# Query bits of the first head straight from PSUM into the stack, and warm products in TensorE's gaps up to the second exponential

## The chip, the cores and the metric

One core of one Trainium2 chip. The metric is the device time of one execution in microseconds (us) on that core. For each run the mean clock granted to TensorE over the execution is also known.

## The reference, cut to what matters

Attention over 4 batches, 8 heads, 768 positions, head width 64, in which a query sees only keys of the same hash bucket, and then a mixture of experts over its result.

```python
q_bits = (np.einsum('bhsd,dk->bhsk', q, proj) > 0)      # 6 bits for each position
k_bits = (np.einsum('bhsd,dk->bhsk', k, proj) > 0)
q_bucket = np.sum(q_bits * powers, axis=-1)             # ... k_bucket likewise
mask = q_bucket[:, :, :, None] == k_bucket[:, :, None, :]
scores = np.where(mask, scale * np.matmul(q, k.transpose(0, 1, 3, 2)), -1e9)
attn = np.exp(scores - np.max(scores, axis=-1, keepdims=True))
attn = attn / (np.sum(attn, axis=-1, keepdims=True) + 1e-09)
out = np.matmul(attn, v)
# ... then gating over 8 experts, relu(x @ w1) @ w2
```

## The kernel before

The mask is not applied to the scores. The bits are stacked as seven more rows below the 64 rows of k and q, so that one matmul with 71 rows gives a score that is far below zero where the buckets differ. Work goes in groups of four heads; a unit is a block of 128 keys of one head. Group 0 is prepared by `at_once()` before the loop:

```python
def at_once():
    bt = wk.tile([P, 2, S], F16, tag="t16", name="bt0")
    # ... hash_twice(): products of the transposed k or q with the hash table, into PSUM tile d["pr" + name]
    def move(name, h):                       # bits from bt into the stack, one half of the positions each
        for x in range(2):
            p = 64 * h + 32 * x
            pin(nc.vector.tensor_copy(d[name][D:KR, h, x * HT:(x + 1) * HT],
                                      bt[p:p + NB + 1, "kq".index(name), 0:HT]))
    # ... put(): bits of heads 2 and 3 to DRAM, from where SyncE fetches them
    for name in "kq":
        # ... transposes on VectorE, placements on ScalarE
        hash_twice(name, 1)
        warm_up(7 if name == "q" else 2)
        # ...
    k_, q_ = bt[:, 0, 0:HT], bt[:, 1, 0:HT]
    pin(nc.vector.tensor_scalar(k_, d["prk"][:, 0, 0:HT], 0.0, 0.5, op0=Alu.is_gt, op1=Alu.subtract))
    pin(nc.vector.tensor_scalar(k_, k_, BIG, None, op0=Alu.mult))
    move("k", 0)
    put("k")
    pin(nc.vector.tensor_scalar(q_, d["prq"][:, 0, 0:HT], 0.0, qoff[:, 0:1], op0=Alu.is_gt, op1=Alu.subtract))
    move("q", 0)
    put("q")
    place("q", 1, 1, nc.vector.tensor_copy)
    # ...
```

`warm_up(n)` issues n products of a tiny constant into a PSUM tile that nobody reads; they only keep TensorE busy. The later groups get their bits through DRAM, with transfers that SyncE issues in order, and the main loop runs one unit of scores ahead of the values:

```python
def prepare(n):                              # n > 0; a generator, run in pieces between units
    # ...
    put_bits()                               # bits to DRAM
    stack("k", 2)                            # rows of k, SBUF to SBUF
    # ...
    for h in range(1 if n < 3 else 0, 2):
        get_bits("k", h)                     # waits until the bits have landed in DRAM
        get_bits("q", h)
    stack("k", 3)
    stack("q", 2)
    get_bits("k", 2)
    # ...
    if n == 1:
        fetch(2, "kq")
        load_w(0, 1, pin=True, half=0)
    cast_v()
# ...
pts = {0: scores(*units[0])}
for u in range(len(units) + 1):
    if u < len(units):
        # ... pieces of prepare(n + 1)
        if u + 1 < len(units):
            pts[u + 1] = scores(*units[u + 1])       # two matmuls, then one exponential on ScalarE
    # ...
    if u > 0:
        values(*units[u - 1], pts.pop(u - 1))        # six matmuls; every sixth unit: normalisation on VectorE
```

The softmax here doesn't subtract the row's maximum and nothing guards it: scores larger than these inputs give would overflow.

## Time and profile before

| | kernel before |
|---|---|
| median of three first runs | 768.26 us (768.13 to 768.45) |
| the run that was profiled | 769.97 us, mean granted clock 0.995 |
| span in that profile | 768.3 us |
| TensorE (PE), ScalarE (ACT), VectorE (DVE), GpSimd (POOL) busy | 98%, 67%, 74%, 41% |

TensorE is busy nearly throughout, so what can be won is a gap at the beginning, where the first scores wait for their inputs, or clock.

Below, e0, e1, ... are the exponentials on ScalarE, one for each unit, and q is the moment at which q has arrived from DRAM (the third transpose on VectorE starts).

### The profile page before, as it was taken

Reading aid. Unit: us, or ns where it says so; the run is one execution under the profiler, and the core shown is the slowest. Engines: PE = TensorE matmul, PEld = TensorE weight load, DVE = VectorE, ACT = ScalarE, POOL = GpSimd, SP = SyncE. Lnnn points to the kernel's source line nnn. Section 1 sums busy time; section 2 is a strip of 40 time slices with the busy share of each in tenths; the row PEclk is TensorE's granted clock in tenths of the full one; section 3 lists DMA queues with packets and bytes.
Section 4 is the critical chain, followed back from the end, with each engine's and each line's share of the span. In section 5 each row is a group of like instructions: output and inputs, shape, how many; then the busy total and the mean of one; then the engine's idle time right before and its main releaser. Section 6 shows DMA issues by size and latency. Waiting matters only on the chain.

```text
span 768.3 us, 16720 instructions
## 1 busy us (share of the span) xinstructions
PE 749.8 (98%) x6285; PEld 518.2 (67%) x6285; DVE 565.6 (74%) x1261; ACT 515.1 (67%) x1027; POOL 318.6 (41%) x327
## 2 busy tenths in 40 slices
PE   8999999999999999999999999999999999999997
PEld 3665666566655667777777777777777777777664
DVE  6587766767579677777777777777777777777774
ACT  5886786678655777766666666666666666666661
POOL 6756444448300333434343334433543344324222
PEclk9899999999999999999999999999999999999999
DMA  7778448651030464676477647654964496443335
GB/s 229 191 199 188 133 113 212 150 144 41 2 55 1 83 110 84 112 136 110 83 132 130 118 89 137 119 104 83 164 118 90 91 169 113 84 83 83 83 83 138
DMA packets 41569, 88.08 MB, mean 115 GB/s; under 512 B 7232, under 2 KB 21840, under 8 KB 41488
## 3 DMA queue, kind: packets, MB, share of 16 engines
q0 software_dynamic: 27168, 69.49, 46.9%
q1 hardware_dynamic: 13324, 16.48, 8.1%
q10 hardware_dynamic: 996, 1.05, 0.6%
q8 instruction: 49, 0.80, 0.5%
q14 instruction: 32, 0.26, 0.1%
HBM read 53.05 MB, written 7.08 MB: 78 GB/s over the span
## 4 chain that ended last, share of the span: by engine, by line
PE 84%; ACT 7%; DVE 6%; issue 1%; DMA 1%; SPq 0%; ACTq 0%; DVEq 0%
PE a L824 18%; PE a L250 18%; PE d L824 13%; PE y L250 9%; PE st L567 6%; ACT pt L570 4%; PE d L250 4%; PE hp L644 4%; PE num L583 3%; PE yp L659 3%; PE pr L406 1%; PE hp L325 1%; PE yp L309 1%; ACT acc L241 1%; DVE hT L833 1%
## 5 line engine op out<-in xcount | busy, mean ns | idle before, releaser
L833 DVE CUSTOM_DVE_ANT_0 hT<-d,u 128x384 f16<-128x384 f32 x336 | 185.1, 552 | 96.7 <-ACT u L829 95.3
L254 ACT ACTIVATE vt<-a,p 128x256 f32<-128x256 f32 x324 | 153.6, 474 | 148.2 <-PE a L250 147.9
L570 ACT ACTIVATE pt<-st 128x768 f16<-128x768 f32 x192 | 147.4, 809 | 45.1 <-PE st L567 44.4
L829 ACT COPY u<-a 128x384 f32<-128x384 f32 x336 | 161.2, 480 | 23.4 <-PE a L824 19.8
L289 POOL DMA_DIRECT2D acc<-vt x72 | 62.0, 861 | 267.2 <-ACT vt L254 114.0
L250 PEld LDWEIGHTS <-hT 128*128 128x128 f16 x1296 | 126.3, 97 | 50.5 <-DVE hT L833 0.8
L250 PE MATMUL a<-t,hs 128*128 128x256 f16 x972 | 145.8, 273 | 2.2 <-ACT vt L254 1.0
L250 PEld LDWEIGHTS <-hs 128*128 128x128 f16 x972 | 94.8, 98 | 38.5 <-issue 2.8
L824 PEld LDWEIGHTS <-t 128*128 128x128 f16 x896 | 87.7, 98 | 36.4 <-issue 0.6
L824 PE MATMUL d<-xd,t 128*128 128x384 f16 x448 | 109.4, 326 | 0.3 <-DVE hT L833 0.3
L824 PE MATMUL a<-xT,s 128*128 128x384 f16 x448 | 109.4, 326 | 0.2
L567 PE MATMUL st<-qs,ks 71*128 71x384 f16 x384 | 95.8, 330 | 5.1 <-ACT pt L570 3.0
L250 PE MATMUL y<-t,hT 128*128 128x256 f16 x648 | 97.1, 272 | 0.0
L258 DVE SCALAR_TENSOR_TENSOR acc<-y,p,acc 128x256 f32<-128x256 f32 x162 | 77.3, 477 | 11.4 <-PE y L250 11.4
L134 POOL TENSOR_TENSOR t<-t 128x1024 f16<-128x1024 f16 (+1 forms) x39 | 81.9, 2108 | 0.1
L583 PEld LDWEIGHTS <-pt 128*128 128x128 f16 x1152 | 61.5, 98 | 27.0 <-issue 1.9
L824 PEld LDWEIGHTS <-s 128*128 128x128 f16 x672 | 65.5, 98 | 17.7 <-issue 2.5
L583 PE MATMUL num<-va,pt 128*128 128x65 f16 x1152 | 67.4, 195 | 0.3 <-ACT pt L570 0.3
L863 ACT ACTIVATE hT<-a 128x384 f16<-128x384 f32 x112 | 54.1, 483 | 1.8 <-PE a L824 1.7
L824 PE MATMUL a<-xd,s 128*128 128x384 f16 x224 | 54.3, 323 | 0.8 <-ACT u L829 0.8
L824 PE MATMUL d<-xT,t 128*128 128x384 f16 x224 | 54.7, 326 | 0.0
L824 PE MATMUL a<-xT,t 128*128 128x384 f16 x224 | 54.7, 326 | 0.0
(120 smaller groups left out, 946.8 us busy)
## 6 DMA issues: line engine op xcount, KB each, us to landing
acc<-vt POOLq DMA_DIRECT2D x72, 512.0 KB, 4.6
t<-in_moe_w_dram POOLq DMA_DIRECT2D x26, 512.0 KB, 8.0
v<-in_v_dram POOLq DMA_DIRECT2D x28, 192.0 KB, 5.6
out_dram<-acc SPq DMA_DIRECT2D x78, 64.0 KB
acc<-in_k_dram POOLq DMA_DIRECT2D x6, 768.0 KB, 6.1
acc<-in_q_dram POOLq DMA_DIRECT2D x6, 768.0 KB, 12.6
t<-in_moe_w_dram POOLq DMA_DIRECT2D x3, 1024.0 KB, 11.9
ks<-t SPq DMA_DIRECT2D x60, 48.0 KB
```

What stands on the lines that cost most here:

```text
L134: pin(nc.gpsimd.tensor_tensor(o[:, sl], x[:, sl], y[:, sl], op=op))
L250: pin(nc.tensor.matmul(dst, hq[hn][:, fo, :], wq[wn][:, fo, :], start=first and fo == 0, stop=fo == FH - 1, skip_group_check=True))
L254: pin(nc.scalar.activation(out=vt[:, k], in_=a, func=Act.Copy, scale=p))
L258: pin(nc.vector.scalar_tensor_tensor(out=dst, in0=src, scalar=p, in1=dst, op0=Alu.mult, op1=Alu.add))
L289: pin(nc.gpsimd.dma_start(out=acc[:, b, i], in_=vt, accum_op=Alu.add))
L567: pin(nc.tensor.matmul(st[:, i, 0:HT], d["k"][0:KR, h, kt * P:(kt + 1) * P], d["q"][0:KR, h, i * HT:(i + 1) * HT], start=True, stop=True))
L570: pin(nc.scalar.activation(out=pt, in_=st[:, :, 0:HT], func=Act.Exp, scale=scale))
L583: pin(nc.tensor.matmul(num[:, j * (D + 1):(j + 1) * (D + 1)], pf[:, j * P:(j + 1) * P], va[:, h, kt, :], start=(kt == 0 and j == 0), stop= ...
L824: pin(nc.tensor.matmul(bk, wq[wn][:, do, f * P:(f + 1) * P], xq[xn][:, do, :], start=first and do == 0, stop=do == 1, skip_group_check=True))
L829: pin(nc.scalar.copy(t, bk))
L833: pin(add(TENSOR_ADD_SAT, out=dst, in0=bk, in1=u, s0=3e38, s1=0.0))
L863: pin(nc.scalar.activation(out=hT[:, f, hi], in_=a, func=Act.Relu))
```

## The change

It has two intents. The bits of the first head of q, which the first scores wait for, are to come from PSUM by two small compares instead of one full compare and two copies. And TensorE's gaps up to the second exponential are to be filled with products, so that its clock doesn't drop just when it becomes the bound.

```diff
                 hash_twice(name, 1)
-                warm_up(7 if name == "q" else 2)
+                warm_up(9 if name == "q" else 4)
 ...
             put("k")
+            for x in range(2):
+                sl = slice(32 * x, 32 * x + NB + 1)
+                pin(nc.vector.tensor_scalar(d["q"][D:KR, 0, x * HT:(x + 1) * HT], d["prq"][sl, 0, 0:HT], 0.0, qoff[sl, 0:1],
+                                            op0=Alu.is_gt, op1=Alu.subtract))
             pin(nc.vector.tensor_scalar(q_, d["prq"][:, 0, 0:HT], 0.0, qoff[:, 0:1], op0=Alu.is_gt, op1=Alu.subtract))
-            move("q", 0)
             put("q")
 ...
+            if u < 2:
+                warm_up(3 - u)
             if u + 1 < len(units):
                 pts[u + 1] = scores(*units[u + 1])
```

## The prediction

> **What bounds the kernel now.** I read the page first (busy shares and slices), then the clock by stretches, the timeline of the first 40 us, the chain of waits there, and the transfers. The page:
>
> ```profile
> PE 749.8 (98%) x6285; PEld 518.2 (67%) x6285; DVE 565.6 (74%) x1261; ACT 515.1 (67%) x1027; POOL 318.6 (41%) x327
> ...
> PEclk9899999999999999999999999999999999999999
> ```
>
> TensorE is nearly always busy; nothing in the MoE part (from about 200 us) is touched by the change. The second digit of the clock row, 8, is the one odd place: the slice 19.2 to 38.4 us. All that the change edits lies before 17 us, so the whole effect is a shift of what comes after, if later waits let it through. Busy times and clock in stretches of 3.41 us, cut at the edges where the clock record changes:
>
> ```profile
> 9.64:13.05 3.41, 3.07 (x23) 0.92 (x23) 3.21 (x11) 3.23 (x5) 1.98 (x3) 1.00 1.07 270
> 13.05:16.47 3.42, 1.95 (x18) 1.00 (x17) 3.28 (x6) 1.89 (x4) 3.21 (x5) 1.00 1.02 346
> 16.47:19.88 3.41, 3.41 (x31) 2.39 (x29) 3.33 (x6) 2.25 (x3) 2.57 (x4) 0.50 0.32 66
> 19.88:23.29 3.41, 3.41 (x32) 2.52 (x30) 1.74 (x3) 2.43 (x3) 3.21 (x5) 0.50 0.17 43
> 23.29:26.70 3.41, 3.41 (x46) 1.72 (x44) 1.69 (x4) 2.26 (x3) 3.41 (x7) 1.00 0.91 192
> ```
>
> (Columns: stretch, length, busy of PE, PEld, DVE, ACT, POOL with counts, granted clock, DMA share, GB/s.) In 13.05 to 16.47 us TensorE is busy only 1.95 of 3.42 us; in the next two stretches, 6.83 us, its clock is 0.50. There PE has no idle time left: it is the bound at half speed, and ScalarE's exponentials wait for it:
>
> ```profile
> 14.52 0.65 PE L567 MATMUL st<-qs,ks 71*128 71x384 f16 x3 [0.43 <-DVE qs L461]
> 14.88 2.21 ACT L570 ACTIVATE pt<-st 128x768 f16<-128x768 f32 x3 [1.53 <-PE st L567]
> 17.35 0.81 ACT L570 ACTIVATE pt<-st 128x768 f16<-128x768 f32 x1 [0.25 <-PE st L567]
> 18.61 0.81 ACT L570 ACTIVATE pt<-st 128x768 f16<-128x768 f32 x1 [0.46 <-PE st L567]
> ...
> 23.73 1.51 ACT L570 ACTIVATE pt<-st 128x768 f16<-128x768 f32 x2 [0.47 <-PE st L567]
> ```
>
> The exponentials e3 to e8 start at 17.35, 18.61, 19.89, 21.17, 22.44 and 23.73: a pitch of 1.276 us. At the full clock ScalarE itself sets the pitch: fifteen in 11.02 us from 32.33, 0.735 each. What leads to the first exponential is VectorE:
>
> ```profile
> 12.55 0.62 DVE L490 TENSOR_SCALAR bt<-pr,qoff 128x384 f16<-128x384 f32 x1
> 13.21 1.27 DVE L461 COPY qs<-bt 7x384 f16<-7x384 f16 x2
> 14.50 1.06 DVE L446 CAST qs<-acc 32x768 f16<-32x768 f32 x1
> ```
>
> The query bits go from PSUM into bt, and two copies put them into the stack qs; only the end of the second (14.49) frees the second matmul of the first score block (14.52).
>
> **What the Trainium skill says.** "TensorE: Matmul & The Clock Gate", Part 1, has the array at half clock unless it was busy, judged in free-running windows of 3413 ns, with two states only. The trace agrees: 16.47 to 23.29 is two such windows at exactly 0.50. It gives no share of busy time as the threshold; here 57% (1.95/3.42) dropped it, while 2.75 of 3.41 us (81%, 30.12 to 33.53) kept it. It also says the window's phase does not start with the kernel, yet the three timed runs differ by 0.32 us in all, so I take the cold stretch to be the same in each. "SBUF — State Buffer", Who interferes with whom, has VectorE and GpSimd share one port pair under an exclusive lock. The trace agrees: the same 7x384 copy takes about 0.26 us for the key bits (0.53 for two at 11.99), but 0.47 and 0.78 for the query bits, when GpSimd casts v from 12.73. "VectorE: DVE Perf Modes", Why PSUM operands drop a tier, says that a PSUM source cannot use both ports. So a read of PSUM should not meet that lock: the 128x384 one at 12.55 took 0.62, and the 64x384 one of a later group 0.62 too, so rows do not count.
>
> **Part 1, the bits.** Removed: two copies, 13.21 to 14.48. Added: two 7x384 compares from PSUM ahead of the full one. Each costs by its length of 384 about 0.62, pitch 0.66 (12.55 to 13.21). They run 12.55 to 13.17 and 13.21 to 13.83, and the full compare 13.87 to 14.49. So VectorE is back where it was at 14.49, the rest of its queue (placement 14.50, group 1's transposes 18.01 to 21.57) does not move, but the second half of the query stack is there at 13.83 in place of 14.49: 0.66 us. The first exponential moves from 14.88 to about 14.2. One counter-effect: the second score block takes the PSUM buffer which the full compare still reads, so it can't start before 14.5.
>
> **Part 2, warm products.** A warm one takes 0.216 of a stream (seven span 1.69 us at 11.62 with the last one's tail). Two more after the key hash run from 8.97 to about 10.0; the query hash started at 9.92 and its second half waited for VectorE at 10.84 anyway: free. Nine after the query hash last from 11.62 to about 13.7, under the wait for the bits. Then three (0.65) between score blocks 0 and 1, two (0.43) between 1 and 2. Worked through: block 0's second matmul 13.88 to 14.05; three products to 14.70; block 1 to 15.03, e1 at about 15.2 rather than at e0's end of 15.03 (0.17 paid to the products); two products to 15.46; block 2 to 15.8, e2 at 16.0, where it is ScalarE's turn. The first values then run to 16.2 and block 3 to 16.5; e3 starts at about 16.75, not 17.35: 0.6 us.
>
> PE is then busy about 3.1 of the 3.42 us of that window (9 products' last 0.6, three score blocks with tails 1.1, five products 1.1, values 0.3), far above the 1.95 that dropped the clock. So I expect 1.00 throughout. At full clock a unit costs PE 0.33 (scores) + 0.18 (values) + 0.16 (the three ident fillers), 0.67 us, just under 0.735. The five pitches e3 to e8 shrink from 1.276 to 0.735: 5 x 0.541 = 2.7 us. Sum at e8: 0.6 + 2.7 = 3.3 us.
>
> **What of it survives.** Group 1's transposes end at 21.57 unchanged. The hash of group 1 reads them at 24.58 and 25.97 now, at 21.3 and 22.7 afterwards: just behind, so no stall. From there VectorE's chain (bits, moves, normalisation, ending in the turn at 31.39) moves with PE; its last piece
>
> ```profile
> 30.32 1.02 DVE L604 TENSOR_TENSOR xn<-nv,rn 128x384 f16<-128x384 f32 x1
> 31.39 0.51 PE L610 MATMUL xp<-ident,xn 128*128 128x128 f16 x6 [0.37 <-DVE xn L604]
> ```
>
> meets GpSimd's cast of v (29.33 on) and takes 1.02 where its fellows take 0.56; 3.3 us earlier it escapes, which may give 0.3 to 0.5 us more. Against that, transfers do not move: group 1's v, the next k and q and half of w1 are issued by GpSimd from 22.45, after its casts of the unmoved transposes, and fill the engines until about 37. The bits of group 1's second head go out to DRAM behind them and are fetched at 35.96; the last packets of that fetch end between 37.5 and 38.0. Scores of that head start at 41.11 now; 3.3 to 3.7 us earlier is 37.4 to 37.8, exactly there. So this wait takes what the shift has above about 3.3, perhaps 0.5 more. Beyond, the next batch of GpSimd transfers starts with the shifted VectorE, and from 66 us PE is near saturated, so the shift stays. I take 0.1 to 0.2 off for new small waits: 768.26 - 3.15 = 765.1 us.
>
> **Rivals.** (a) The clock drops all the same, or one window later, because the gate weighs rows or phases I don't see: only 0.6 us is left, perhaps less with nine more products on PE: about 767.7. For it: PE at full occupancy in 16.47 to 19.88 did not win the clock back at 19.88, so busy time alone is not the measure. Against: the new products are dense, full-width ones. (b) Transfers fixed in time eat the shift: the second head's bits at 38, or the two stack rows of group 2 which SyncE issues in order from 42.74 whatever PE does: 766 to 766.5. For: the DMA share is about 1 in 13 to 16, 27 to 37 and 46 to 54 us. Against: the other landings that I followed keep some 2 us beyond the shift. (c) The products delay e1 and e2 and VectorE's longer hold of PSUM delays block 1, so that nothing is gained before e3: worth 0.3 us at most, since ScalarE catches up. (d) Shift and freed contention add up unhindered: 764.4.
>
> **Range and chances.** (b) in part and (d) span 764.3 to 766.9; (a) lies outside and gets about one in ten. A 2% change is 15 us; the waits that the change touches add up to less than a third of that, so faster or slower by 2% is practically excluded.
>
> **What would show it.** Right: clock 1.00 from 13 to 27 us; e0 at about 14.2, e3 at 16.8, e8 at 20.4; two qs compares of 0.6 us at 12.55; transposes still at 18.0; first turn near 28; PE at 66 us doing what it did at 69. Wrong: a 0.50 stretch anywhere after 6.2 us, compares that take over 0.8 us, or a wait of PE or ScalarE near 38 us for a bits fetch longer than 0.5 us. If the time is above 767, step 2 failed; if between, the survival argument.

## The result, and the profile after

| | before | after |
|---|---|---|
| median (range), 4 runs each | 768.36 us (768.13 to 769.69) | 766.88 us (766.81 to 767.12) |
| span in the profile | 768.3 us | 765.1 us |

The ratio after/before is 0.9978, 95% interval 0.996 to 0.9995: the same at 2%, with a small gain that the interval just keeps apart from none. A ratio here is the mean time of one kernel's runs over that of the other's of the same rounds, so it is not quite the ratio of the medians quoted. All outputs are right.

The page of the changed kernel, the busy shares and the clock in 40 slices; the 8 in the second slice has become a 9:

```profile
PE 747.5 (98%) x6294; PEld 517.2 (68%) x6294; DVE 567.4 (74%) x1261; ACT 514.0 (67%) x1027; POOL 318.3 (42%) x327
...
PEclk9999999999999999999999999999999999999999
```

The changed kernel by stretches of 3.41 us (same columns as in the prediction; the grid of the stretches lies elsewhere in this run):

```profile
8.06:11.47 3.41, 3.34 (x32) 0.78 (x28) 2.55 (x8) 3.18 (x5) 2.37 (x4) 1.00 1.15 214
11.47:14.88 3.41, 3.41 (x19) 1.48 (x16) 3.18 (x8) 2.50 (x4) 2.17 (x4) 1.00 0.98 350
14.88:18.30 3.42, 3.42 (x49) 2.54 (x47) 3.28 (x6) 3.25 (x6) 3.03 (x6) 1.00 0.77 185
```

PE (the first busy figure) has no gap left and the clock stays at 1.00. Its timeline of ScalarE and VectorE answers the prediction's lines:

```profile
12.61 1.25 DVE L492 TENSOR_SCALAR qs<-pr,qoff 7x384 f16<-7x384 f32 x2
13.89 0.62 DVE L494 TENSOR_SCALAR bt<-pr,qoff 128x384 f16<-128x384 f32 x1
...
14.27 0.81 ACT L573 ACTIVATE pt<-st 128x768 f16<-128x768 f32 x1 [0.86 <-PE st L570]
15.25 6.68 ACT L573 ACTIVATE pt<-st 128x768 f16<-128x768 f32 x9 [0.17 <-PE st L570]
```

Two compares from PSUM take 1.25 us (expected 2 x 0.62), e0 starts at 14.27 (expected about 14.2), and nine exponentials run in 6.68 us without a wait, where before ScalarE waited for PE ahead of each one from e3 to e8.

The span fell by 3.2 us, nearly what the sum of the prediction says. The medians fell by 1.48 us. That is the puzzle: one of the two kernels must show something in its profile which its ordinary runs don't have.

### The profile page after: what moved, and what is told of

Read it like the earlier page. It is cut to its first block, busy times and chain, and to the rows that moved or that the text cites. A ratio compares the mean times of both kernels' runs of the same rounds, so it can differ in the third digit from the quotient of the medians. Undisturbed runs are those within 1.5% of the kernel's fastest.

```text
span 765.1 us, 16738 instructions
## 1 busy us (share of the span) xinstructions
PE 747.5 (98%) x6294; PEld 517.2 (68%) x6294; DVE 567.4 (74%) x1261; ACT 514.0 (67%) x1027; POOL 318.3 (42%) x327
## 4 chain that ended last, share of the span: by engine, by line
PE 84%; DVE 6%; ACT 6%; issue 1%; DMA 1%; SPq 0%; ACTq 0%; DVEq 0%
PE a L829 18%; PE a L250 18%; PE d L829 13%; PE y L250 9%; PE st L570 6%; PE d L250 4%; ACT pt L573 4%; PE hp L647 4%; PE yp L662 3%; PE num L586 3%; PE pr L406 1%; PE hp L325 1%; PE yp L309 1%; ACT acc L241 1%; DVE hT L838 1%
## 5 line engine op out<-in xcount | busy, mean ns | idle before, releaser
L570 PE MATMUL st<-qs,ks 71*128 71x384 f16 x384 | 94.0, 325 | 3.6 <-ACT pt L573 2.4
```

The source lines that it names most:

```text
L570: pin(nc.tensor.matmul(st[:, i, 0:HT], d["k"][0:KR, h, kt * P:(kt + 1) * P], d["q"][0:KR, h, i * HT:(i + 1) * HT], start=True, stop=True))
```

## The experiments

Theory P: whether the clock drops near 13 us depends on where the free-running window of the clock happens to lie in a run. The profiled run of before had a cold stretch, many ordinary runs do not, and what the change wins is mostly that no run has it. Rival H: every run of before has a cold stretch, the ordinary one of a single window of 3.41 us, the other of two. The quoted texts call them by these letters. Later letters are W, that transfers whose times do not shift eat what the change gains, and J, that late inputs make the slow runs and the clock only follows.

The segments of the traces, in us; q and the span are absolute, the rest is counted from q:

| trace | q | e0 | e3 | e8 | e17 | e40 | end | span |
|---|---|---|---|---|---|---|---|---|
| before | 8.88 | 6.00 | 8.46 | 14.84 | 23.44 | 42.74 | 759.38 | 768.3 |
| control (before again) | 8.51 | 6.14 | 8.29 | 11.96 | 20.17 | 39.48 | 756.07 | 764.6 |
| bits_only | 9.08 | 5.34 | 7.62 | 11.29 | 19.81 | 39.95 | 756.63 | 765.7 |
| warm_only | 9.02 | 6.22 | 8.69 | 12.36 | 20.51 | 39.95 | 756.66 | 765.7 |
| after | 8.94 | 5.34 | 7.81 | 11.48 | 19.97 | 39.52 | 756.16 | 765.1 |
| after_again | 8.61 | 5.34 | 7.81 | 11.48 | 19.88 | 40.76 | 757.42 | 766.0 |
| after_third | 8.60 | 5.33 | 7.80 | 11.47 | 19.77 | 39.15 | 755.63 | 764.2 |
| cold | 8.54 | 5.84 | 7.99 | 13.07 | 21.63 | 40.93 | 757.45 | 766.0 |
| loop_only | 8.35 | 5.33 | 7.80 | 11.47 | 19.84 | 42.61 | 759.23 | 767.6 |

And the times. "Cold runs" counts runs with a mean clock of 0.998 or less. One 3.41 us window at half clock lowers the mean over some 766 us by 0.0022, so this is an estimate, from the clock, of which runs had a window beyond the first ramp; only profiled runs show where it lay. The count is generous at 0.998: the traces also have a half-clock stretch at the very end, up to 2.15 us of it inside the span (cold), which alone lowers the mean by 0.0014, and before has runs at 0.998 as short as 766.11 us. With 0.997 or less as the limit the counts are 10 of 37 for the kernel before (control included), 4 of 5 for cold, 1 of 5 for loop_only and for w1_late, 0 of 6 for before_order, and still none for the changed kernel.

| kernel | chip | median us (range) | ratio to before, 95% | cold runs |
|---|---|---|---|---|
| before | 11 | 768.15 (766.11 to 771.82) | | 5 of 11 |
| control | 11 | 768.18 (766.29 to 768.73) | 0.9998 [0.9975, 1.0021] | 3 of 6 |
| bits_only | 11 | 766.96 (766.48 to 770.98) | 0.9993 [0.9966, 1.0021] | 2 of 6 |
| warm_only | 11 | 767.43 (766.96 to 771.43) | 0.9995 [0.9969, 1.002] | 1 of 6 |
| after_again | 11 | 767.06 (766.65 to 767.75) | 0.9982 [0.9961, 1.0003] | 0 of 6 |
| before | 2 | 766.35 (765.77 to 769.09) | | 5 of 9 |
| cold | 2 | 768.55 (767.71 to 769.45) | 1.0017 [0.9999, 1.0036] | 5 of 5 |
| loop_only | 2 | 766.55 (766.18 to 770.76) | 1.0009 [0.9982, 1.0035] | 4 of 5 |
| sp_order | 2 | 766.72 (766.33 to 766.77) | 0.9993 [0.9973, 1.0012] | 1 of 5 |
| w1_late | 2 | 767.64 (766.92 to 768.28) | 1.0006 [0.9988, 1.0024] | 2 of 5 |
| before | 4 | 766.57 (766.0 to 769.56) | | 4 of 11 |
| after_third | 4 | 766.28 (765.79 to 767.16) | 0.9991 [0.9977, 1.0005] | 0 of 6 |
| order_again | 4 | 766.32 (765.89 to 766.45) | 0.999 [0.9976, 1.0004] | 0 of 6 |
| bits_first | 4 | 766.35 (766.16 to 766.87) | 0.9992 [0.9977, 1.0007] | 1 of 6 |
| before_order | 4 | 766.97 (766.22 to 768.44) | 1.0001 [0.9985, 1.0017] | 3 of 6 |

### control: the kernel before, unedited

> The kernel before, unchanged, against itself. The time that a run is given stood 1.67 us over the profile's span both for the profiled execution of before (769.97 against 768.3) and of the change (766.81 against 765.1), so the three early runs of before (768.13 to 768.45) had spans near 766.6 and were not like the profiled one, which held a 6.83 us stretch at half clock. Theory P (phase): whether the half-clock stretch happens depends on where the free-running window falls, so the runs come in two kinds, ordinary ones near 768.3 with a granted clock of about 0.998 to 1.000 and no half-clock stretch, and some near 769.7 to 770.0 with 0.994 to 0.996. Rival H (half): every execution has a cold stretch, the ordinary one of a single window of 3.41 us (clock about 0.002 lower than the changed kernel's), the other of two. A profile of an ordinary run decides it. Ratio 1.000 either way, with scatter up to 0.2%.

Its runs scatter by 2.4 us, and the profiled one (766.29 us) has no cold stretch. Its stretches, to be held against the prediction's:

```profile
11.57:14.98 3.41, 2.34 (x11) 0.82 (x10) 3.22 (x7) 1.91 (x3) 2.42 (x3) 1.00 0.97 395
14.98:18.39 3.41, 2.88 (x45) 2.31 (x45) 3.29 (x6) 3.41 (x6) 2.85 (x5) 1.00 0.61 142
18.39:21.81 3.42, 3.42 (x55) 2.41 (x52) 3.38 (x6) 3.42 (x5) 2.90 (x4) 1.00 0.19 48
```

The same code with the same gap of PE keeps its clock here, because the grid lies at 11.57 and 14.98 instead of 13.05 and 16.47: the gap is spread over two windows, 2.34 and 2.88 us busy, instead of 1.95 and 3.41. In the table e3 to e8 takes 3.67 us instead of 6.38, and the span is 764.6 us instead of 768.3. So the whole 3.2 us between the two profiles that the prediction compares is no more than what two executions of the kernel before differ by (3.7). H falls, and P holds as to the window. P's two kinds of runs, though, do not part by time as it expected: 768.24 us at a clock of 1.000 and 768.12 at 0.999 are as slow as runs with a cold window, so something other than the clock also costs up to 2 us in this kernel. Those runs have no trace.

Counting PE's busy time over every place of the window in this trace, the windows that begin between about 11.9 and 13.2 us are 53 to 60% busy: some 40% of all places. In the changed kernel's trace none from 10 to 20 us is under 98%.

### bits_only and warm_only: one part of the change each

```diff
  bits_only: the change, with
-                warm_up(9 if name == "q" else 4)
+                warm_up(7 if name == "q" else 2)
-            if u < 2:
-                warm_up(3 - u)
  warm_only: the kernel before, with
-                warm_up(7 if name == "q" else 2)
+                warm_up(9 if name == "q" else 4)
+            if u < 2:
+                warm_up(3 - u)
```

> Only the compare straight from PSUM, no new warm products. Theory P: the change's ordinary gain of 1.4 to 1.5 us comes from the bits (0.66 us at the first exponential) and what follows from the shift; ordinary runs at 766.9 to 767.6, and some slower runs of about 1.5 us more stay, clock 0.995. Rival H: the bits alone give 0.6 us, ordinary runs at 767.7, all with a cold window.

> Only the nine new warm products, the query bits go through the two copies as before. Theory P: no gain in ordinary runs, 768.2 to 768.6 (the three products between the first score blocks now delay the second block, some 0.2 us), but no slow runs with a clock near 0.995 at all. Rival H: the products take away the cold window of each run: 766.9 to 767.4.

The bits alone bring e0 forward to 5.34 after q, against 5.84 to 6.22 in the five traces with the old bits (the four in the table, and before_order with 5.92): 0.66 us between the two first profiles, as predicted. The products alone leave e0 where it was and cost at e3: 8.69 against 8.29. With the bits, the products' cost is 7.81 - 7.62 = 0.19 us (0.17 was the estimate).

Neither part alone moves the mean clear of noise: the ratios are 0.9993 and 0.9995, with intervals from 0.997 to 1.002 (nor does the whole change in this batch, 0.9982 with 0.9961 to 1.0003). Each kernel still has slow runs (769.78 and 770.98 us, clock 0.997; 771.43, clock 0.997), against P's expectation of none near 0.995 for warm_only. In this batch only the two together had none, but 0 of 6 against 2 and 1 of 6 does not show that both are needed. The traces speak against it: counted over every place of the window that begins between 10 and 20 us, PE is nowhere less than 81% busy in bits_only and 80% in warm_only, where control falls to 53%. Each part alone closes most of the gap, so these slow runs may have another cause, as the one of loop_only below has.

### after_again and after_third: the changed kernel, unedited

> The changed kernel again, on the same chip. Both theories: 766.8 to 767.1, clock 0.998 to 1.000 in every run, no half-clock stretch after the first 6 us in the profile, whatever the phase. If it shows a run near 768.5 with a clock near 0.995, the products do not protect against every phase.

> The changed kernel in the same rounds as its variants. Theory: no early cold stretch in any run; a wait of 0 to 1.6 us before e30 or e36, and where that leaves a window under about 57% busy, a late cold window. 766.6 to 767.8, median 767.0; should a run at 769 to 771 with a clock near 0.997 appear, it is the late one.

With the first four runs that makes 16 runs of the changed kernel on three occasions, none cold, from 765.79 to 767.75 us. The kernel before had 17 cold ones of 37 (5 of 11, 3 of 6 as control, 5 of 9, 4 of 11). But after_again shows the second thing: to e17 it is the equal of after, and then it loses 1.2 us before e40. The groups of PE's timeline there:

```profile
43.26 0.49 PE L631 MATMUL hp<-xT,t 128*128 128x384 f16 x2
44.94 0.48 PE L570 MATMUL st<-qs,ks 71*128 71x384 f16 x2 [1.19 <-ACT pt L573]
```

and of ScalarE's:

```profile
41.89 2.25 ACT L573 ACTIVATE pt<-st 128x768 f16<-128x768 f32 x3 [0.58 <-PE st L570]
45.52 1.65 ACT L573 ACTIVATE pt<-st 128x768 f16<-128x768 f32 x2 [1.37 <-PE st L570]
```

PE's wait of 1.19 us is put down to an exponential, but ScalarE had nothing to do from 44.14 (41.89 + 2.25) to 45.52, so it cannot have released PE at 44.94. What else this score block needs are the rows and bits of its head, which SyncE had begun to fetch; in loop_only, below, the profile names such a fetch in the same place. That it is the same here is inferred.

### cold: the kernel before with no product after the query hash

```diff
-                warm_up(7 if name == "q" else 2)
+                warm_up(0 if name == "q" else 2)
```

> The kernel before without its seven warm products after the query hash, so that TensorE has a hole from 11.7 to 13.7 us and any window that falls there is thin: in the trace of control, windows of 3.41 us that begin between 11.9 and 13.2 us are only 53 to 60% busy with the products, about 40% of all phases; without them nearly every phase has one below that. Theory P (phase of the window decides, and a cold stretch costs 3.7 us): nearly all runs show a clock of 0.994 to 0.996, and spans of 768 to 770, so a median near 770, and the profile a half-clock stretch of 6.8 us that begins between 13.5 and 17 us, with e3 to e8 at a pitch of 1.27. Rival J (the slow runs of before are late inputs, the clock only follows): the same mixture as before, 766 to 771, median 768.

All five runs are cold by the table's limit, on a chip on which 5 of 9 of the kernel before were (4 of 5 against 1 of 9 by the stricter one), and the median is 2.2 us above before's. So the gap makes the clock drop. The size that P expected, two windows and a median near 770, did not come. The stretches of its profile:

```profile
9.50:12.91 3.41, 1.70 (x16) 0.31 (x16) 3.17 (x12) 3.31 (x5) 2.33 (x3) 1.00 1.06 296
12.91:16.32 3.41, 2.05 (x19) 1.23 (x20) 3.29 (x6) 2.15 (x4) 3.17 (x6) 1.00 1.02 347
16.32:19.73 3.41, 3.41 (x34) 2.56 (x33) 3.35 (x5) 2.49 (x4) 2.57 (x5) 0.50 0.25 59
19.73:23.14 3.41, 3.41 (x53) 2.33 (x51) 3.07 (x6) 3.11 (x5) 3.34 (x5) 1.00 0.25 64
```

One window is cold, not two, and e3 to e8 takes 5.08 us, 1.41 more than warm; two windows cost 2.71. Two things stay open. The window 9.50 to 12.91 was only 50% busy and the next was still at full clock, while 60% in 12.91 to 16.32 dropped it. And here one fully busy window won the clock back, while before needed two. The busy share as the profile has it does not decide either in every case.

### loop_only: the bits and the loop's products, but only seven after the query hash

```diff
  the change, with
-                warm_up(9 if name == "q" else 4)
+                warm_up(7 if name == "q" else 2)
```

> The changed kernel without the four products added after the hashes; the five between the first score blocks stay, and the bits. Theory P: the thin windows begin at 11.9 to 13.2 us, where bits_only with the original seven was 81% busy in its profile, so the five loop products are what closes the hole behind 13.7 us; no run below 0.998, median 766.6 to 767.3, like the changed kernel. If a run near 0.997 and 769 to 771 appears as in bits_only, the added hash products are needed too, or such runs have another cause than the hole.

The expectation failed: 769.29 and 770.76 us are among the five runs. But its profile shows that a slow run needn't come from the gap at 13 us. To e17 it is as the changed kernel; the cold stretch lies at 46:

```profile
45.41 0.48 PE L570 MATMUL st<-qs,ks 71*128 71x384 f16 x2 [1.61 <-DMA ks<-ds]
```

```profile
42.43:45.85 3.42, 1.55 (x20) 0.83 (x17) 2.11 (x6) 1.76 (x3) 0.95 (x2) 1.00 1.06 204
45.85:49.26 3.41, 3.41 (x28) 2.06 (x26) 1.95 (x5) 1.74 (x3) 0.58 (x1) 0.50 1.10 241
49.26:52.67 3.41, 3.41 (x48) 2.49 (x46) 2.47 (x5) 3.14 (x5) 3.17 (x6) 1.00 0.99 266
```

PE waits 1.61 us for a fetch of bits, is busy 45% of that window, and loses the clock in the next; the end comes 3.07 us later from q than in after (759.23 against 756.16). So a late transfer can cost its own wait and a cold window on top. In after_again the window in which the wait fell, by its own grid 43.07 to 46.48, was busy 2.22 of 3.41 us (65%), and the clock stayed.

### sp_order and w1_late: is it SyncE's order, or the weights' transfer?

The bits of group 1 go out to DRAM and are fetched again by SyncE, which issues in order and stands until the write has landed. sp_order puts the rows of head 3 of k behind the bits of head 2; w1_late issues the half of w1 after the casts of v.

```diff
  sp_order: the change, with                 w1_late: the change, with
-        stack("k", 3)                            if n == 1:
+        if n > 1:                                    fetch(2, "kq")
+            stack("k", 3)                   -        load_w(0, 1, pin=True, half=0)
         stack("q", 2)                            cast_v()
         get_bits("k", 2)                    +    if n == 1:
         get_bits("q", 2)                    +        load_w(0, 1, pin=True, half=0)
+        if n == 1:
+            stack("k", 3)
```

> The changed kernel, but for group 1 SyncE issues the third head's query rows and bits before the fourth head's key rows. Theory W (what the change gains on VectorE is given back where heads 2 and 3 of group 1 wait for transfers whose times do not shift: e36 came 1.35 us late in after_again, and SyncE's first fetch of bits was at 29.2 us in control but 33.4 to 35.3 in the others): the wait before e36 goes or shrinks by up to 1.2 us; median 0.2 to 0.5 us below the changed kernel's 767.0, and the slowest runs 1 us lower. Rival: the transfers are slowed by the engines' load and not by the order of issue, no change.

> The changed kernel, with the first half of the first expert's w1 (1 MB) loaded after group 1's v is cast, not before. It is wanted at e34 only. Theory W with load as the cause: the bits of group 1 no longer wait behind that megabyte, SyncE's first fetch of them moves from 33.4 to 35.3 us to about 31, the waits before e30 and e36 are gone, 0.3 to 1.0 us less than the changed kernel, median 766.1 to 766.7. Rival: the load then meets the next batch of k and v from 38 us on and e34 or group 2 waits for it: same or slower, 767 to 768.

sp_order loses nothing before e36, and its five runs spread by only 0.44 us, but the trace has a new wait further on, 0.95 us before e54, and the median is not below before's on the same chip. The order gives the wait back later:

```profile
58.51 0.48 PE L573 MATMUL st<-qs,ks 71*128 71x384 f16 x2 [0.95 <-ACT pt L576]
```

w1_late fails: the first fetch is issued at 33.73 us, as in after (33.40), and the median is 767.64. The half of w1 isn't what delays the write. One of its five runs has a clock of 0.996 (768.28 us), although its preparation of group 0 is the changed kernel's; it has no trace, so where that window lay is not known.

### order_again, bits_first, before_order: is there a version that beats both?

order_again is sp_order on another chip; bits_first is sp_order with the rows of heads 1 of groups 1 and 2 behind the writing of the bits; before_order is the kernel before with sp_order's edit.

```diff
  bits_first: sp_order, and in prepare()
-        stack("k", 1)            # likewise for "q"
+        if n > 2:
+            stack("k", 1)
 ...
         put_bits()
+        if n < 3:
+            stack("k", 1)
+            stack("q", 1)
```

> The changed kernel with the third head's rows and bits ahead of the fourth's, again. Theory W: median 766.4 to 766.8 and all runs within 0.6 us, below the changed kernel of the same rounds by 0.2 to 0.4. Rival (the tight five runs of sp_order were luck): median and scatter as the changed kernel's.

> As order_again, and for groups 1 and 2 SyncE also sends the bits out before the second head's rows, so that they do not queue behind them: in sp_order's trace the fetch of group 1's bits was issued at 33.8 us, 8.5 us after they were sent, and of group 2's at 55.6 with a wait of 0.95 us on PE before e54. Theory W: fetches at about 29 to 31 and 52 us, the waits before e30, e36 and e54 all gone, 765.3 to 766.2, about 1 us less than the changed kernel. Rival (second head's rows, now later, become the wait, or SyncE stands still until the bits are ready and delays everything behind): no gain, 766.7 to 767.5.

> The kernel before with only the third head's rows and bits ahead of the fourth's. Two causes of slow runs are then told apart: the early cold stretch stays (runs with a clock of 0.994 to 0.998 and 767.5 to 769), the wait before e36 with the late cold window goes (no run above 769.5; before had 770.98 and 771.82 among eleven). Median 0 to 0.5 us below the kernel before of the same rounds. If runs above 770 stay as frequent, the late wait is not what makes them.

order_again gives the narrowest scatter (0.56 us in six runs against 1.37 of after_third), but its median is that of after_third, not the 0.2 to 0.4 us lower that was expected. bits_first does what it should in SyncE's timeline, with the write sooner and the fetch at 29.61 where after has 33.40:

```profile
24.61 0.35 SPq L422 DMA_DIRECT2D ds<-bt  x1
29.61 0.42 SPq L425 DMA_DIRECT2D ks<-ds  x1
```

and its trace has no wait of PE above 0.35 us between 26 and 62 us. Still the median is 766.35: the expected 1 us is not there. In before_order the cold runs stay (3 of 6). So no version clearly beats the changed kernel. All six runs of before_order stay below 769.5 us, as expected, but so do all six of control, so this does not settle what makes runs above 770. In these three batches, runs of 769.2 us and more were 8 of 54 of before, control, bits_only, warm_only and loop_only, and none of 23 with the other SyncE order; since the changed kernel itself had none of 16, this only suggests that the order helps.

## Why the prediction was right and where it was not

The measured median, 766.88, lies 0.02 us inside the edge of the stated range (765.1, with 764.3 to 766.9), and the class was right. That it lies inside is luck: the gain was 1.48 us and not 3.15, because the starting time did not belong to the profile that the sum was taken from. Taken off the profiled run's own 769.97 us, the same sum gives 766.82, against 766.81 for the profiled run of after. The steps:

**The bits.** Right: e0 0.66 us earlier from q in the pair of profiles, two compares in 1.25 us, VectorE's queue behind them all but unmoved (the transposes of group 1 start 9.27 us after q, in before 9.13, in control 9.26).

**The warm products.** Right: PE's gap is closed and no run of 16 is cold. What is shown for these steps is the pair of profiles, one with two cold windows and one with none. e3 to e8 shrank from 6.38 to 3.67 us, 2.71 against the predicted 2.7; e8 came 3.36 us earlier from q against 3.3. From e54 to the end every trace takes 705.8 to 706.2 us, so what is left at 59 us stays to the end, as predicted, and the pair of profiles ends 3.22 us apart from q against 3.15. So close a match is partly chance, since three traces of the changed kernel end between 755.63 and 757.42 us from q.

**The premise that failed** is the prediction's "the three timed runs differ by 0.32 us in all, so I take the cold stretch to be the same in each". The Trainium skill, "TensorE: Matmul & The Clock Gate", Part 1, says of this window that it is free-running and that the number of cold matmuls at a kernel's start varies between runs of one kernel with its phase; the prediction had read that the phase is free and overruled it by three runs that happened to agree. The control shows the same for a stretch in mid-kernel: one kernel, two grids, 764.6 and 768.3 us. The sign was there before any run: 769.97 us for the profiled run, of span 768.3, is not a run of 768.26. Subtracting the sum from 768.26 took 3.15 us off runs that were already 1.7 us shorter than the profiled one. Those runs have no clock on record; whether they had one cold window, or none and some other loss, stays open.

**What the change is worth** follows from the two kinds of runs. On chip 4 the kernel before's warm runs (clock 0.999 and above) have a mean of 766.46 us (seven runs) and its cold ones of 768.34 (four); after_third, all warm, has 766.34. Compared warm with warm, the change gains 0.1 us. Of the gain of 0.8 us in the mean (767.14 against 766.34), the other 0.7 us are the cold runs that it no longer has (four of eleven, 1.88 us each). On chip 11, after_again's mean is 767.08, and before with control together has 767.29 warm (nine runs at 0.999 and above) and 769.13 cold (eight).

**Why the 0.5 us at e8 is not kept in a warm run.** From q, after is 0.48 us ahead of control at e8, 0.20 at e17 and no longer ahead at e40. VectorE's and PE's timelines of control:

```profile
23.64 0.55 DVE L414 TENSOR_SCALAR bt<-pr 64x384 f16<-64x384 f32 x1 [0.58 <-PE pr L406]
...
27.14 0.56 DVE L604 TENSOR_TENSOR xn<-nv,rn 128x384 f16<-128x384 f32 x1
27.75 0.51 PE L610 MATMUL xp<-ident,xn 128*128 128x128 f16 x6
```

and of the changed kernel:

```profile
23.58 0.55 DVE L414 TENSOR_SCALAR bt<-pr 64x384 f16<-64x384 f32 x1
...
27.36 0.56 DVE L607 TENSOR_TENSOR xn<-nv,rn 128x384 f16<-128x384 f32 x1
27.97 0.51 PE L613 MATMUL xp<-ident,xn 128*128 128x128 f16 x6 [0.26 <-DVE xn L607]
```

In control VectorE waits 0.58 us for PE's hash of group 1, and PE waits for nothing at the turn. In the changed kernel PE is early, VectorE has no wait any more, and at the turn it is PE that waits, 0.26 us. VectorE's transposes and normalisation between did not move, so it takes over as the bound: the turn comes 19.24 us after q in control and 19.03 in after. This is the prediction's claim that VectorE's chain "moves with PE", right while PE was cold and late, wrong where it was not.

**The rivals.** (b), transfers that eat the shift, was right in kind. In the changed kernel the write of group 1's bits is issued at 25.90 us and the fetch behind it at 33.40:

```profile
25.90 0.53 SPq L422 DMA_DIRECT2D ds<-bt  x1
33.40 0.27 SPq L425 DMA_DIRECT2D ks<-ds  x1
```

while control has:

```profile
25.16 0.35 SPq L422 DMA_DIRECT2D ds<-bt  x1
29.24 0.27 SPq L425 DMA_DIRECT2D ks<-ds  x1
```

From issue to fetch is 7.50 us against 4.08: the write lands some 3.4 us slower. The Trainium skill, "DMA: Bandwidth & Descriptors", Queues, rings and completion order, has each DMA engine take turns between its queues packet by packet; here the write would share the engines with GpSimd's loads, issued from 22.16 us on in control and 22.61 in after, of which w1 alone was cleared (w1_late).

The slow landing does not belong to the changed kernel alone: before has 7.55 us, cold 8.07, warm_only 7.67. In all fourteen traces it goes by one order. Where the write is issued ahead of GpSimd's load of k for group 2 (control and before_order by 0.19 us, bits_first by 0.34), the fetch follows 4.08 to 5.00 us behind it; where the write is issued after that load, be it by 0.07 us as in after, it follows 7.30 to 9.34 us behind. bits_first moved the write on purpose, by an edit of SyncE's order, and landed on the quick side. That the load of k is the cause was not tested by moving the load.

From e17 to e40 control takes 19.31 us, after 19.55, after_third 19.38 and after_again 20.88, and a run whose bits come very late gets a cold window as well. Rival (a), the clock dropping all the same, did not come true in any run of the changed kernel; of its variants, loop_only and w1_late had one run each at 0.997 or less, loop_only's from a late fetch. (c) was right in size: 0.19 us for the loop's products.

**What stays open**: what exactly makes the gate drop or restore the clock; how much of the slow timed runs of bits_only and warm_only is the gap at 13 us and how much a late transfer, since those runs have no trace; what makes runs of before slow at a full clock; whether moving GpSimd's load of k would speed the write.

## What to carry to other kernels

Before you take a stage of a profile as the ordinary one, compare the profiled run's own time and clock with the times of the other runs, and count how many runs are of its kind; a control of the unedited kernel in the same batch is worth more than a closer look at one trace. When TensorE's gap is some 40% of a clock window, as here, whether it costs is a matter of chance in each run, so judge filler products by the share of slow runs, not by the best ones. What is won ahead of an engine that did not move lasts only until that engine is next waited for.

## What the Trainium skill lacked or had wrong

- "TensorE: Matmul & The Clock Gate" gives no busy share for its gate. Here windows busy 57% (before), 60% (cold) and 45% (loop_only) were followed by half clock, and windows busy 62% (warm_only, 4.22 to 7.63 us), 65% (after_again), 69% (control) and 50% (cold, its first) were not. With the windows laid on each trace's own grid, the fourteen traces show, up to the kernel's last windows, no other that lost the clock and none else below 62% that kept it, so cold's first is the one exception to a limit between 60 and 62%. One fully busy half-clock window restored the clock in cold and loop_only, while before took two.
- The same page puts the ramp at less than 1% of a kernel's span and advises not to fit a cold count. The size agrees (1.4 to 2.7 us directly, of some 766), but between these two kernels such stretches make most of the difference: the cold runs of the kernel before had a mean of 768.34 against 766.46 us of the warm ones on one chip. The first switch to full clock lay anywhere from 3.76 to 6.22 us in the traces.
- "SBUF — State Buffer", Who interferes with whom, was checked and not found wrong. It describes the lock of VectorE against GpSimd as a full block for an instruction; in before the 7x384 copy took 0.25 us alone and 0.47 and 0.77 beside GpSimd's casts, and each of these two ended 0.11 us after a cast did (13.68 after 13.56, 14.47 after 14.36). The loss, 0.2 and 0.5 us, follows what was left of the cast when the copy started, 0.36 and 0.66 us.
